# A transformer layer with dilated local attention: p\*v in 64x32 tiles with 32 queries by 48 keys, and a new order of all operations

## The chip, the cores and the metric

The kernel runs on one core of a Trainium2 chip. The core has five engines with a queue each: TensorE (PE, with its weight loads as PEld), VectorE (DVE), ScalarE (ACT), GpSimd (POOL) and SyncE (SP), which issues most DMAs. The metric is the device time of one execution in microseconds (us), where lower is better.

## What is computed

The input x has 2048 rows of 448 numbers in bf16. Attention has 16 heads of 28, and each query looks at 8 keys: its own position and the 7 that lie 2, 4, ... 14 positions back.

```python
def _A_ref(x, wqkv, wo):
    H = 16; Dh = D // H
    W, dil = 8, 2
    q, k, v = ...                                   # x @ wqkv, by heads
    idx = pos[:, None] - (jnp.arange(W) * dil)[None, :]
    mask = idx >= 0
    logits = jnp.einsum("bhsd,bhswd->bhsw", q, k[idx]) * Dh ** -0.5
    attn = softmax(where(mask, logits, -1e9))
    o = jnp.einsum("bhsw,bhswd->bhsd", attn, v[idx])
    return o.reshape(B, S, D) @ wo

def _B_ref(x, w1, w2, w3, w4):                      # F = 1792
    h = gelu(layernorm(x) @ w1)
    hs = concat(the four quarters of h's columns, shifted by +1, -1, +2, -2 rows) @ w2
    x1 = x + hs
    return x1 + gelu(layernorm(x1) @ w3) @ w4

h = x + _A_ref(layernorm(x), wqkv, wo)
return h + _B_ref(layernorm(h), w1, w2, w3, w4)
```

## The kernel before

The 2048 rows are worked on as four blocks of 512 rows (t = 0 to 3) of four tiles of 128 rows each. A block goes through these phases: **N1** (layernorm of x), **A1** (turning of the normalized rows, then q and k), **V** (v, and its copies to `vw`), **A2** (logits), **S** (softmax, and turning of p), **A3** (p\*v), **O** (times wo, plus x), **B1** (second layernorm) and **M** (times w1, gelu). Then five units of 2, 4, 4, 4 and 2 tiles go through **B2** (times w2 with shifted rows, layernorm as **T**), **W3** (times w3, gelu) and **B3** (times w4, output).

Each phase records its operations, and `arrange` then puts all 912 of them in the order of the list `ORDER`. Each engine executes its own operations strictly in that order, waiting on semaphores for the others. An operation that has an alternative runs on ACT, unless its number is in `OTHER`; then DVE runs it. Evictions from PSUM (`copy`) and normalizations by ACT have such alternatives. Buffers come from pools with fixed numbers: `NBD` for the spread p, `NLN` for normalized rows, `NACT` for turned rows, `NO` for output rows. `NORM`, `STATS` and `POWER` say for each block which engine ('a' ACT, 'v' DVE, 'p' POOL) does the normalizing, the statistics and the power -1/2 of a layernorm.

Most products have a contraction of 448 = 3 x 128 + 64, and are done as pairs of matmuls on the two halves of PE's rows (64x128 tiles). `duo` pairs two output banks: in the first half of the work (s = 0) the upper rows write bank A and the lower rows bank B, in the second half (s = 1) it is the other way round, since two row halves must not write one bank at the same time. That is why the second half waits for the first (`sdeps`). Turning in `transposed` and of p in `phase_A2` is split in two halves for the same reason.

p\*v: after the softmax, `pb` holds p with its 8 weights per query, spread so that turning it by PE gives `pt`, with keys on the partitions: 80 keys (16 before the tile's 64) by queries. For each of the four tiles of a block, DVE multiplies `pt`, broadcast, with a 0/1 mask (`bmask`), which gives `bd_r`: 80 keys by 64 queries for each of 32 (half tile, head) pairs. Then 32 matmuls with `vw` (80 keys by the 32 columns of one head) as weights and 64 columns of `bd_r` as moving operand write one bank, in four column tiles of 32. One eviction brings the bank, with reordered columns, into `actT`. `vw` is written by three or four DMAs per block from `vt`, issued on POOL's queue.

The loads of x, the attention's weights, w1 and w2 are issued by SP in the order in which they are recorded; those of w3 and w4 by POOL. All instructions show the line of the function that emits them (956), so they are told apart by the tiles that they write and read.

Of the kernel before, what the change touches and what calls it, by code (L numbers as in the profile page):

```python
# [6 lines left out]
ALU = mybir.AluOpType  # L7
# [6 lines left out]
NORM = {'N0': 'aava', 'N1': 'avvv', 'B1': 'avvv', 'B2': 'avvvv'}  # L14
STATS = {'N1': 'vvva', 'B1': 'vvav', 'B2': 'avvvv'}
NBD, NLN, NACT, NSM, NO = 3, 2, 4, 1, 3
# [34 lines left out]
"""  # L51
OTHER = """
96 110 502 548 595 596
"""

# [219 lines left out]
def bass_sequential_preLN__sliding_local_dilated__mixer_s_mlp__prompt_kernel(  # L275
# [11 lines left out]
    KW = 80  # L287
# [20 lines left out]
    with ExitStack() as es:  # L308
# [5 lines left out]
        bd_r = sb("bd_r", [KW, NBD, 2048], BF16)  # L314
        vt = sb("vt", [128, 2, 4, 512], BF16)
        vw = sb("vw", [KW, 2, 8, 512], BF16)
        bmask = sb("bmask", [KW, 64], BF16)
# [21 lines left out]
        pb = sb("pb", [128, NSM, NW * KW], BF16)  # L339
# [23 lines left out]
        pt = [arv(A_KV + t * KVB + 4 * KVW, KW, 1024) for t in range(NST)]  # L363
# [58 lines left out]
        def load_rows(chan, dst, src, lo, n, eng="sp", after=()):  # L422

            dma(chan, dst[:, 0:3, :], src[0:384, lo:lo + n].rearrange("(c k) n -> k c n", k=128), 384 * n * 2, eng=eng, after=after)
            return [dma("%sr%d" % (chan, h), dst[64 * h:64 * h + 64, 3, :], src[384:448, lo:lo + n], 64 * n * 2, eng=eng) for h in range(2)][-1]
# [4 lines left out]
        load_rows("wqk", wqkv_s[:, :, 0:2 * D], A_wqkv, 0, 2 * D)  # L430
        load_x(4, 2)
        load_x(6, 2)
        load_rows("wv", wqkv_s[:, :, 2 * D:3 * D], A_wqkv, 2 * D, D)
# [8 lines left out]
        for eng in ("sp", "pool"):  # L442
# [90 lines left out]
        def normalize(kind, i, out_ap, in_ap, summed=False, norm="v"):  # L533
# [6 lines left out]
            return dve("tensor_scalar", **by_dve)  # L540
# [14 lines left out]
        def doubled(ln, lo, n):  # L555
            dve("tensor_copy", out=ln(lambda v: v[:, lo:lo + n, D:512]), in_=ln(lambda v: v[:, lo:lo + n, 384:D]))

        def transposed(ln, how, n=4):
# [5 lines left out]
            w = n // 2  # L564
# [8 lines left out]
            first = []  # L573
            for s in range(2):
                for j in range(w):
                    op = steps([turn(h, j if h == s else w + j, c) for c in range(4) for h in range(2)], meth="transpose")
                    op.sdeps.update(first[-1:] * s)
                    first += [op] * (1 - s)
            for k, b in enumerate(banks):
                copy(a(lambda v, k=k: v[:, w * k:w * k + w, :, :]), b(lambda v: v.bitcast(BF16)[:, 0:512 * w].rearrange("p (i c n) -> p i c n", i=w, c=4)))  # L580
# [19 lines left out]
        def setup():  # L600
# [21 lines left out]
            for w in range(NW):  # L622
                bm = bmask[:].rearrange("p (m e r) -> p m e r", m=4, e=2)
                pool("affine_select", out=bm, in_=bm, pattern=[[16, 4], [1, 2], [DIL, NW]],
                     compare_op=ALU.not_equal, fill=1.0, base=PADK - DIL * w, channel_multiplier=-1)
# [11 lines left out]
        def phase_N1(t):  # L637
            ln = a1_ln[t] = _Tile(P_ln)
            step = 1 if t == 0 else 4
            summed = STATS["N1"][t] == "a"  # L640
            for lo in range(4 * t, 4 * t + 4, step):
# [7 lines left out]
                norms = norms_of("N1", t, 4) if t else NORM["N0"][lo]  # L649
# [5 lines left out]
        def phase_A1(t):  # L655
# [15 lines left out]
            names = ("q0", "q1", "q2", "k0", "k1", "k2")  # L671
# [21 lines left out]
        def phase_V(t):  # L693
# [16 lines left out]
            dma("vwa%d" % sl, vw[PADK:KW, sl, 0:8:2, :], vt[0:64, sl, :, :], 64 * 4096, "pool")  # L710
            dma("vwb%d" % sl, vw[0:KW, sl, 1:8:2, :], vt[48:128, sl, :, :], 80 * 4096, "pool")
            dma("vwc%d" % sl, vw[0:PADK, sl, 2:8:2, :], vt[112:128, sl, 0:3, :], 16 * 3072, "pool")

        def phase_A2(t):
# [31 lines left out]
            row = lambda v, off, step: bass.AP(v, off, [[v.shape[1] * v.shape[2], 128], [step, NW], [16, 4], [DIL, NW], [1, DIL]])  # L746
            dve("tensor_tensor", out=row(pb, sl * NW * KW + DIL, KW + DIL), in0=row(ls, sl * 512, 64),
# [10 lines left out]
            for g, b in enumerate(banks):  # L758
                copy(pt[t].rearrange("p (n r) -> p n r", r=NW)[:, :, 4 * g:4 * g + 4], b(lambda v: v[0:KW, :].rearrange("p (r n) -> p n r", r=4)))
# [238 lines left out]
```

## Time and profile before

| what | us |
|---|---|
| median of 3 runs (198.76 to 199.75) | 199.13 |
| the profiled execution, whole | 199.03 |
| its span, first to last instruction | 197.3 |
| PE busy | 186.4 (95% of the span) |
| DVE busy | 135.9 (69%) |
| ACT busy | 120.0 (61%) |
| POOL busy | 58.3 (30%) |

Busy times are unions of the instructions' durations. A matmul's duration runs from its start until its modelled end, which reaches into the matmuls behind it, so a busy PE isn't a PE at its peak. The clock granted to PE was 1.00 throughout.

### The profile page before, as it was taken

What the parts mean: (1) busy time and instruction counts of PE and PEld (TensorE: products, weight loads), DVE (VectorE), ACT (ScalarE), POOL (GpSimd) and SP (SyncE); (2) the same over time, 40 slices, a digit from 0 to 9 for tenths busy, and PEclk for the clock granted to TensorE, in tenths of its full rate; (3) what the DMA queues carried; (4) which work ended last, traced back from release to release, by engine and by line L of the source; (5) the groups of instructions that cost most, each with busy time, mean ns of one, the idle gap of its engine ahead of it and who ended that gap; (6) DMA issues with size and microseconds to landing.
All of it is one profiled execution on the core that took longest, in us unless ns stands there. A gap on an engine that the chain in (4) does not pass through costs nothing.

```text
span 197.3 us, 5852 instructions
## 1 busy us (share of the span) xinstructions
PE 186.4 (95%) x2532; PEld 97.6 (49%) x2532; DVE 135.9 (69%) x251; ACT 120.0 (61%) x271; POOL 58.3 (30%) x92
## 2 busy tenths in 40 slices
PE   6999998999999989999997999999996999999994
PEld 2474343544435455466553445555453454455672
DVE  4899999999999899999789836099571004302303
ACT  4869999999996989998270365720066023540350
POOL 4333430600002609726292460031076000610000
DMA  5979930370025360186508040004306100300211
GB/s 154 327 213 295 250 90 3 83 148 3 3 44 102 85 121 0 19 312 136 107 20 95 0 94 16 3 0 94 109 0 124 32 0 23 70 10 15 71 60 47
DMA packets 24513, 16.66 MB, mean 84 GB/s; under 512 B 16776, under 2 KB 23240, under 8 KB 24488
## 3 DMA queue, kind: packets, MB, share of 16 engines
q1 hardware_dynamic: 22872, 10.24, 22.5%
q0 software_dynamic: 1616, 6.05, 11.6%
q8 instruction: 20, 0.33, 0.7%
q14 instruction: 5, 0.04, 0.1%
HBM read 7.91 MB, written 1.84 MB: 49 GB/s over the span
## 4 chain that ended last, share of the span: by engine, by line
PE 48%; DVE 27%; ACT 10%; DMA 9%; issue 2%; POOL 1%; SPq 1%; DVEq 0%; POOLq 0%
PE ps L956 48%; DVE qk_r L956 8%; DVE lntm L956 6%; DMA actT<-lntm 5%; DVE bd_r L956 5%; ACT lntm L956 3%; DMA out_dram<-ost 3%; ACT actT L956 2%; ACT arena L956 2%; DVE st L956 2%; DVE arena L956 2%; DMA xin<-in_A_x_dram 1%; ACT vt L956 1%; POOL rs_y L956 1%; DVE ost L956 1%
## 5 line engine op out<-in xcount | busy, mean ns | idle before, releaser
L956 PE MATMUL ps<-actT,arena 64*128 64x512 bf16 (+1 forms) x742 | 70.4, 332 | 4.2 <-DMA actT<-lntm 3.8
L956 ACT ACTIVATE h3T<-ps 128x512 bf16<-128x512 f32 (+1 forms) x70 | 30.7, 521 | 52.6 <-PE ps L956 52.4
L956 PEld LDWEIGHTS ps<-actT,arena 64*128 64x128 bf16 x742 | 34.6, 94 | 34.5 <-DMA actT<-lntm 4.4
L956 PE MATMUL ps<-arena,h3T 64*128 64x448 bf16 (+2 forms) x434 | 45.4, 343 | 0.0
L956 DVE SCALAR_TENSOR_TENSOR ost<-ps,mrs,arena 128x448 bf16<-128x448 f32 (+1 forms) x17 | 10.9, 651 | 38.7 <-PE ps L956 33.7
L956 ACT ACTIVATE arena<-ps 128x512 bf16<-128x512 f32 (+4 forms) x70 | 33.1, 510 | 6.5 <-PE ps L956 5.7
L956 PEld LDWEIGHTS ps<-arena,h3T 64*128 64x128 bf16 (+1 forms) x434 | 23.6, 94 | 18.3 <-ACT h3T L956 0.2
L956 DVE TENSOR_TENSOR qk_r<-arena 128x4096 bf16<-128x4096 bf16 (+1 forms) x16 | 31.7, 2013 | 0.4 <-ACT arena L956 0.3
L956 POOL TENSOR_TENSOR arena<-arena,xin 128x448 f32<-128x448 f32 x16 | 20.0, 1272 | 18.3 <-DVE lntm L956 18.3
L956 POOL TENSOR_TENSOR rs_y<-rs_x,mhalf 128x4 f32<-128x4 f32 (+1 forms) x9 | 9.3, 1035 | 44.9 <-DVE rs_x L956 44.8
L956 ACT ACTIVATE actT<-ps 128x512 bf16<-128x512 f32 (+2 forms) x27 | 17.6, 691 | 3.9 <-PE ps L956 3.6
L956 DVE TENSOR_TENSOR bd_r<-arena,bmask 80x2048 bf16<-80x2048 bf16 x16 | 18.9, 1214 | 0.0
L956 DVE SCALAR_TENSOR_TENSOR arena<-xin,rs_y,ps 128x448 f32<-128x448 bf16 x16 | 10.4, 669 | 10.3 <-PE ps L956 10.3
L956 POOL TENSOR_TENSOR mrs<-nm,rs_y 128x4 f32<-128x4 f32 x4 | 8.4, 2102 | 27.1 <-ACT rs_y L956 21.9
L956 DVE BATCH_NORM_STATS2 st<-xin 128x6 f32<-128x448 bf16 x24 | 13.9, 612 | 2.0 <-DMA xin<-in_A_x_dram 1.8
L956 PE MATMUL ps<-wo_s,actT 64*128 64x448 bf16 x128 | 14.7, 350 | 0.2 <-ACT xin L956 0.2
L956 PE MATMUL ps<-w_s,arena 64*128 64x448 bf16 (+1 forms) x128 | 14.3, 349 | 0.0
L956 PE MATMUL ps<-actT,w_s 64*112 64x512 bf16 x112 | 13.5, 377 | 0.3 <-DMA actT<-lntm 0.3
L956 POOL DMA_DIRECT2D vw<-vt x15 | 9.1, 606 | 14.5 <-PE ps L956 9.4
L956 PE MATMUL ps<-arena,actT 64*128 64x448 bf16 x112 | 13.1, 350 | 0.1
L956 DVE TENSOR_SCALAR lntm<-arena,mv,rs_y 128x448 bf16<-128x448 f32 x14 | 9.2, 699 | 3.1 <-POOL rs_y L956 3.1
L956 PEld LDWEIGHTS ps<-actT,w_s 64*112 64x112 bf16 x112 | 7.4, 127 | 4.3 <-ACT actT L956 0.4
(74 smaller groups left out, 178.3 us busy)
## 6 DMA issues: line engine op xcount, KB each, us to landing
out_dram<-ost SPq DMA_DIRECT2D x15, 112.0 KB, 1.8
arena<-in_B_w_dram POOLq DMA_DIRECT2D x1, 1568.0 KB, 8.1
arena<-in_B_w_dram POOLq DMA_DIRECT2D x1, 1344.0 KB, 7.3
vw<-vt POOLq DMA_DIRECT2D x4, 320.0 KB, 3.9
vw<-vt POOLq DMA_DIRECT2D x4, 256.0 KB, 4.0
xin<-in_A_x_dram SPq DMA_DIRECT2D x2, 448.0 KB, 5.8
xin<-in_A_x_dram SPq DMA_DIRECT2D x3, 224.0 KB, 4.7
arena<-in_A_wqkv_dram SPq DMA_DIRECT2D x1, 672.0 KB, 5.3
```

Of the source, the lines that this page charges most:

```text
L956: inst = getattr(eng, meth)(**kw)
```

## The change

p\*v is cut differently. A block of 64 queries by 80 keys becomes two blocks of 32 queries by 48 keys (16 before, 32 own), one on the partitions 0 to 47, the other on 64 to 111. PE works on them as 64x32 tiles, eight side by side: two row halves, each into its own bank, by four column tiles. `bd_r` now has 128 partitions and holds two tiles of 128 rows per buffer, so a block has two spreading operations instead of four, and two groups of 128 matmuls with 32 columns instead of four groups of 32 matmuls with 64. The matmuls' moving operand is read in the order in which the eviction wants it, and the evictions copy runs of 32 columns, one per row half. p is turned with 128 columns of weights. `vw` is written by five or six DMAs per block.

The turns (of layernorm output and of p) write one bank per row half, and no longer wait between halves. v's weights are loaded first. The pairs of q and k are formed anew. The number of `bd_r` buffers goes from 3 to 2 and of output buffers from 3 to 5. All normalizations have ACT as their first choice, and the statistics of B1 of the first block are done by ACT (sums of squares). The first four tiles are normalized in two pairs instead of one by one. `ORDER` is new, and 41 operations run on DVE by `OTHER` instead of 6.

```diff
-NORM = {'N0': 'aava', 'N1': 'avvv', 'B1': 'avvv', 'B2': 'avvvv'}
-STATS = {'N1': 'vvva', 'B1': 'vvav', 'B2': 'avvvv'}
-NBD, NLN, NACT, NSM, NO = 3, 2, 4, 1, 3
+NORM = {'N0': 'aaaa', 'N1': 'aaaa', 'B1': 'aaaa', 'B2': 'aaaaa'}
+STATS = {'N1': 'vvva', 'B1': 'avav', 'B2': 'avvvv'}
+NBD, NLN, NACT, NSM, NO = 2, 2, 4, 1, 5
...
 OTHER = """
-96 110 502 548 595 596
+99 110 115 125 209 210 211 235 236 237 238 266 301 304 329 331 332 356 357 358 380 421 445 474 493 531 563 564 565 566
+587 588 595 652 654 655 729 801 803 866 867
 """
+FIRST = ((0, 2), (2, 2))
+RQ = 'sp'
+RV = 'act'
...
-    KW = 80
+    QB = 32
+    KB = PADK + QB
...
-        load_rows("wqk", wqkv_s[:, :, 0:2 * D], A_wqkv, 0, 2 * D)
+        load_rows("wv", wqkv_s[:, :, 2 * D:3 * D], A_wqkv, 2 * D, D, last=RV)
+        load_rows("wqk", wqkv_s[:, :, 0:2 * D], A_wqkv, 0, 2 * D, last=RQ)
         load_x(4, 2)
         load_x(6, 2)
-        load_rows("wv", wqkv_s[:, :, 2 * D:3 * D], A_wqkv, 2 * D, D)
...
             def turn(h, il, c):
-                b = banks[il // w]
                 part = (TOP, BOT)[h]
-                return (h, dict(out=b(lambda v, lo=il % w * 512 + c * 128 + 64 * h: v.bitcast(BF16)[:, lo:lo + 64]),
+                return (h, dict(out=banks[h](lambda v, lo=(4 * il + c) * 64: v.bitcast(BF16)[:, lo:lo + 64]),
                                 in_=ln(lambda v, il=il, c=c: v[part, il, 128 * c:128 * c + 128]), identity=ident[part, part]), 64)
...
-                op.sdeps.update(first[-1:] * s)
...
-            names = ("q0", "q1", "q2", "k0", "k1", "k2")
+            names = ("q0", "k0", "q1", "k1", "q2", "k2")
...
-            dma("vwa%d" % sl, vw[PADK:KW, sl, 0:8:2, :], vt[0:64, sl, :, :], 64 * 4096, "pool")
-            dma("vwb%d" % sl, vw[0:KW, sl, 1:8:2, :], vt[48:128, sl, :, :], 80 * 4096, "pool")
-            dma("vwc%d" % sl, vw[0:PADK, sl, 2:8:2, :], vt[112:128, sl, 0:3, :], 16 * 3072, "pool")
+            for name, to, even, lo, hi in (("a", PADK, 0, 0, QB), ("b", 64, 0, PADK, 64), ("c", 0, 1, 64 - PADK, 64 + QB), ("d", 64, 1, 64 + PADK, 128)):
+                dma("vw%s%d" % (name, sl), vw[to:to + hi - lo, sl, even:8:2, :], vt[lo:hi, sl, :, :], (hi - lo) * 4096, "pool")
+            dma("vwe%d" % sl, vw[0:PADK, sl, 2:8:2, :], vt[112:128, sl, 0:3, :], 16 * 3072, "pool")
...
-            first = steps([turn(h, h, r) for r in range(4) for h in range(2)])
-            steps([turn(h, 1 - h, r) for r in range(4) for h in range(2)]).sdeps.add(first)
+            steps([turn(h, r) for r in range(NW) for h in range(2)])
...
-            for il in range(4):
+            for pair in range(2):
                 bd = _Tile(P_bd)
-                b = _Tile(P_bank)
-                dve("tensor_tensor", block=True, out=bd(lambda v: v.rearrange("p (n g r) -> p n g r", g=8, r=NW)),
+                banks = [_Tile(P_bank), _Tile(P_bank)]
+                dve("tensor_tensor", block=True, out=bd(lambda v: v.rearrange("p (n g r) -> p n g r", g=4, r=NW)),
...
+                at = (i8 // 2 * 8 + 2 * c + i8 % 2) * QB
+                specs.append((("matmul", dict(out=banks[half](lambda v, j=j, at=at: v[32 * j:32 * j + 32, at:at + QB].rearrange("p (m r e) -> p m r e", m=2, e=DIL)),
+                                              lhsT=vw[part, sl, 4 * pair + i8, (4 * c + j) * 32:(4 * c + j) * 32 + 32],
+                                              rhs=bd(lambda v, part=part, lo=(16 * i8 + 4 * c + j) * QB: v[part, lo:lo + QB].rearrange("p (m e r) -> p m r e", m=2, e=DIL)), start=True, stop=True)),
+                              (QB, "q", 4 * half + j)))
...
-                copy(a(lambda v, il=il: v[:, il, :, :].rearrange("p c n -> p (c n)").rearrange("p (m r e) -> p m r e", r=NW, e=2)),
-                     b(lambda v: v.rearrange("p (m e r) -> p m r e", r=NW, e=2)))
+                for half, b in enumerate(banks):
+                    copy(a(lambda v, lo=2 * pair, half=half: v[:, lo:lo + 2, :, :].rearrange("p i c (u h q) -> p (i c u) h q", u=2, h=2)[:, :, half, :]),
+                         b(lambda v: v.rearrange("p (u q) -> p u q", q=QB)))
```

More of the change, by code (lines that the diff above doesn't have):

```diff
@@ L313, in bass_sequential_preLN__sliding_local_dilated__mixer_s_mlp__prompt_kernel @@
         qk_r = sb("qk_r", [128, 2, 4096], BF16)
-        bd_r = sb("bd_r", [KW, NBD, 2048], BF16)
+        bd_r = sb("bd_r", [128, NBD, 2048], BF16)
         vt = sb("vt", [128, 2, 4, 512], BF16)
-        vw = sb("vw", [KW, 2, 8, 512], BF16)
-        bmask = sb("bmask", [KW, 64], BF16)
+        vw = sb("vw", [128, 2, 8, 512], BF16)
+        bmask = sb("bmask", [128, QB], BF16)
         lntm = sb("lntm", [128, NLN, 4, 512], BF16)
@@ L338, in bass_sequential_preLN__sliding_local_dilated__mixer_s_mlp__prompt_kernel @@
         indj = ls[:, NSM - 1, 0:40].bitcast(BF16).rearrange("p (c h) -> p c h", c=5)
-        pb = sb("pb", [128, NSM, NW * KW], BF16)
+        pb = sb("pb", [128, NSM, NW * 128], BF16)
         ost = sb("ost", [128, NO, D], BF16)
@@ L362, in bass_sequential_preLN__sliding_local_dilated__mixer_s_mlp__prompt_kernel @@
         kr = [arv(A_KV + t * KVB + 3 * KVW, 128, PADK + 256) for t in range(NST)]
-        pt = [arv(A_KV + t * KVB + 4 * KVW, KW, 1024) for t in range(NST)]
+        pt = [arv(A_KV + t * KVB + 4 * KVW, 128, 1024) for t in range(NST)]
         maskrow = arv(A_KV + (NST - 1) * KVB, 1, 512)
@@ L420, in load_x, with load_rows @@
             return dma("x%d" % i, xin[:, i:i + n, :], xv[:, i:i + n, :], 128 * n * D * 2)
-        def load_rows(chan, dst, src, lo, n, eng="sp", after=()):
+        def load_rows(chan, dst, src, lo, n, eng="sp", after=(), last=None):
             dma(chan, dst[:, 0:3, :], src[0:384, lo:lo + n].rearrange("(c k) n -> k c n", k=128), 384 * n * 2, eng=eng, after=after)
-            return [dma("%sr%d" % (chan, h), dst[64 * h:64 * h + 64, 3, :], src[384:448, lo:lo + n], 64 * n * 2, eng=eng) for h in range(2)][-1]
+            return [dma("%sr%d" % (chan, h), dst[64 * h:64 * h + 64, 3, :], src[384:448, lo:lo + n], 64 * n * 2, eng=last or eng) for h in range(2)][-1]
         S.tag = "load"
@@ L441, in bass_sequential_preLN__sliding_local_dilated__mixer_s_mlp__prompt_kernel @@
         dma("w4", w4_s, B_w4.rearrange("(f k) n -> k f n", k=128), D * F * 2, eng="pool", after=[late])
-        for eng in ("sp", "pool"):
+        for eng in ("sp", "pool", "act"):
             loads = [op for op in S.ops if op.tag == "load" and op.eng == eng]
@@ L539, in normalize @@
                              alts=[("dve", [("tensor_scalar", by_dve)])])
-            return dve("tensor_scalar", **by_dve)
+            return dve("tensor_scalar", True, **by_dve)
         def norms_of(kind, t, n):
@@ L555, in doubled @@
         def doubled(ln, lo, n):
-            dve("tensor_copy", out=ln(lambda v: v[:, lo:lo + n, D:512]), in_=ln(lambda v: v[:, lo:lo + n, 384:D]))
+            dve("tensor_copy", True, out=ln(lambda v: v[:, lo:lo + n, D:512]), in_=ln(lambda v: v[:, lo:lo + n, 384:D]))
         def transposed(ln, how, n=4):
@@ L563, in transposed @@
                 return a
-            w = n // 2
             banks = [_Tile(P_bank), _Tile(P_bank)]
             def turn(h, il, c):
-                b = banks[il // w]
                 part = (TOP, BOT)[h]
-                return (h, dict(out=b(lambda v, lo=il % w * 512 + c * 128 + 64 * h: v.bitcast(BF16)[:, lo:lo + 64]),
+                return (h, dict(out=banks[h](lambda v, lo=(4 * il + c) * 64: v.bitcast(BF16)[:, lo:lo + 64]),
                                 in_=ln(lambda v, il=il, c=c: v[part, il, 128 * c:128 * c + 128]), identity=ident[part, part]), 64)
[L573 to L576, printed above, removed]
-                    op.sdeps.update(first[-1:] * s)
-                    first += [op] * (1 - s)
-            for k, b in enumerate(banks):
-                copy(a(lambda v, k=k: v[:, w * k:w * k + w, :, :]), b(lambda v: v.bitcast(BF16)[:, 0:512 * w].rearrange("p (i c n) -> p i c n", i=w, c=4)))
+            for il in range(n):
+                steps([turn(h, il, c) for c in range(4) for h in range(2)], meth="transpose")
+            for h, b in enumerate(banks):
+                copy(a(lambda v, lo=64 * h: v[:, 0:n, :, lo:lo + 64]), b(lambda v: v.bitcast(BF16)[:, 0:256 * n].rearrange("p (i c n) -> p i c n", i=n, c=4)))
             return a
@@ L621, in setup @@
             pool("memset", ap=bmask[:], constant=0.0)
[L622 to L625, printed above, removed]
+            bm = bmask[:].rearrange("p (m e r) -> p m e r", m=2, e=2)
+            for base in [64 * half + PADK - DIL * w for half in range(2) for w in range(NW)]:
+                pool("affine_select", out=bm, in_=bm, pattern=[[16, 2], [1, 2], [DIL, NW]],
+                     compare_op=ALU.not_equal, fill=1.0, base=base, channel_multiplier=-1)
             pool("memset", ap=gT[:, :, 0:2], constant=0.0)
@@ L638, in phase_N1 @@
             ln = a1_ln[t] = _Tile(P_ln)
-            step = 1 if t == 0 else 4
             summed = STATS["N1"][t] == "a"
-            for lo in range(4 * t, 4 * t + 4, step):
+            for lo, step in FIRST if t == 0 else ((4 * t, 4),):
                 for i in range(lo, lo + step):
@@ L648, in phase_N1 @@
                     sums_stats(0, range(lo, lo + step), lambda i: xin[:, i, :], ln, lo % 4)
-                norms = norms_of("N1", t, 4) if t else NORM["N0"][lo]
+                norms = norms_of("N1", t, 4) if t else NORM["N0"][lo:lo + step]
                 rstd(0, lo, step, summed, norms, POWER["N1"][t])
@@ L745, in phase_A2, with turn @@
             dve("reciprocal", out=zs[:, sl, :], in_=zs[:, sl, :])
-            row = lambda v, off, step: bass.AP(v, off, [[v.shape[1] * v.shape[2], 128], [step, NW], [16, 4], [DIL, NW], [1, DIL]])
-            dve("tensor_tensor", out=row(pb, sl * NW * KW + DIL, KW + DIL), in0=row(ls, sl * 512, 64),
-                in1=bass.AP(zs, sl * 64, [[64 * NSM, 128], [8, NW], [2, 4], [0, NW], [1, DIL]]), op=ALU.mult)
+            row = lambda v, off, step, half: bass.AP(v, off, [[v.shape[1] * v.shape[2], 128], [step, NW], [half, 2], [16, 2], [DIL, NW], [1, DIL]])
+            dve("tensor_tensor", out=row(pb, sl * NW * 128 + DIL, 128 + DIL, 64), in0=row(ls, sl * 512, 64, QB),
+                in1=bass.AP(zs, sl * 64, [[64 * NSM, 128], [8, NW], [4, 2], [2, 2], [0, NW], [1, DIL]]), op=ALU.mult)
             banks = [_Tile(P_bank), _Tile(P_bank)]
-            def turn(h, g, r):
+            def turn(h, r):
                 part = (TOP, BOT)[h]
-                return (h, dict(out=banks[g](lambda v: v[0:KW, 128 * r + 64 * h:128 * r + 64 * h + 64]),
-                                lhsT=pb[part, sl, (4 * g + r) * KW:(4 * g + r + 1) * KW], rhs=ident[part, part], start=True, stop=True), 64)
-            first = steps([turn(h, h, r) for r in range(4) for h in range(2)])
-            steps([turn(h, 1 - h, r) for r in range(4) for h in range(2)]).sdeps.add(first)
-            for g, b in enumerate(banks):
-                copy(pt[t].rearrange("p (n r) -> p n r", r=NW)[:, :, 4 * g:4 * g + 4], b(lambda v: v[0:KW, :].rearrange("p (r n) -> p n r", r=4)))
+                return (h, dict(out=banks[h](lambda v: v[:, 64 * r:64 * r + 64]), lhsT=pb[part, sl, r * 128:(r + 1) * 128], rhs=ident[part, part],
+                                start=True, stop=True), 64)
+            steps([turn(h, r) for r in range(NW) for h in range(2)])
+            for h, b in enumerate(banks):
+                copy(pt[t].rearrange("p (n r) -> p n r", r=NW)[:, 64 * h:64 * h + 64, :], b(lambda v: v.rearrange("p (r n) -> p n r", r=NW)))
         def phase_A3(t):
@@ L763, in phase_A3 @@
             sl = t % 2
-            for il in range(4):
+            for pair in range(2):
                 bd = _Tile(P_bd)
-                b = _Tile(P_bank)
-                dve("tensor_tensor", block=True, out=bd(lambda v: v.rearrange("p (n g r) -> p n g r", g=8, r=NW)),
-                    in0=pt[t][:, il * 256:il * 256 + 256].rearrange("p (n r) -> p n r", r=NW).unsqueeze(2).broadcast_to([KW, 32, 8, NW]),
-                    in1=bmask[:].rearrange("p (g r) -> p g r", r=NW).unsqueeze(1).broadcast_to([KW, 32, 8, NW]), op=ALU.mult)
-                mms([(b(lambda v, j=j, lo=128 * c + 64 * a2: v[32 * j:32 * j + 32, lo:lo + 64]),
-                      vw[:, sl, 2 * il + a2, (4 * c + j) * 32:(4 * c + j) * 32 + 32],
-                      bd(lambda v, lo=(16 * a2 + 4 * c + j) * 64: v[:, lo:lo + 64]), True, True, 64, j)
-                     for c in range(4) for a2 in range(2) for j in range(4)])
-                copy(a(lambda v, il=il: v[:, il, :, :].rearrange("p c n -> p (c n)").rearrange("p (m r e) -> p m r e", r=NW, e=2)),
-                     b(lambda v: v.rearrange("p (m e r) -> p m r e", r=NW, e=2)))
+                banks = [_Tile(P_bank), _Tile(P_bank)]
+                dve("tensor_tensor", block=True, out=bd(lambda v: v.rearrange("p (n g r) -> p n g r", g=4, r=NW)),
+                    in0=pt[t][:, pair * 512:pair * 512 + 512].rearrange("p (n r) -> p n r", r=NW).unsqueeze(2).broadcast_to([128, 64, 4, NW]),
+                    in1=bmask[:].rearrange("p (g r) -> p g r", r=NW).unsqueeze(1).broadcast_to([128, 64, 4, NW]), op=ALU.mult)
+                specs = []
+                for i8 in range(4):
+                    for c in range(4):
+                        for half in range(2):
+                            for j in range(4):
+                                part = slice(64 * half, 64 * half + KB)
+                                at = (i8 // 2 * 8 + 2 * c + i8 % 2) * QB
[3 more added lines that the diff above has]
+                                              (QB, "q", 4 * half + j)))
+                S.group("pe", [x for x, _ in specs], pe=[y for _, y in specs])
+                for half, b in enumerate(banks):
+                    copy(a(lambda v, lo=2 * pair, half=half: v[:, lo:lo + 2, :, :].rearrange("p i c (u h q) -> p (i c u) h q", u=2, h=2)[:, :, half, :]),
+                         b(lambda v: v.rearrange("p (u q) -> p u q", q=QB)))
```

62 rows, old and new, of the table ORDER are left out of this document.

## The prediction

> **What bounds the kernel now.** I read the page's busy shares, then busy time by stage, then the chain that ended last, then groups, waits and the timeline at the steps that change. First the page: share of the span and count per engine, and the span in 40 slices of 4.93 us.
>
> ```profile
> span 197.3 us, 5852 instructions
> ...
> PE 186.4 (95%) x2532; PEld 97.6 (49%) x2532; DVE 135.9 (69%) x251; ACT 120.0 (61%) x271; POOL 58.3 (30%) x92
> ...
> PE   6999998999999989999997999999996999999994
> ...
> DVE  4899999999999899999789836099571004302303
> ACT  4869999999996989998270365720066023540350
> ```
>
> PE's 95% overstates: the streaming time of its matmuls (2.38 columns a ns, as 512-column matmuls on one tile follow each other every 215 ns, divided by the tiles that run side by side) sums to 172 us. Until slice 18 (about 90 us) DVE and ACT are as full as PE. By stage (PE, PEld, DVE, ACT, POOL busy, each with its count):
>
> ```profile
> 8.75:35.42 26.67, 25.82 (x359) 12.46 (x361) 26.09 (x42) 23.85 (x58) 8.89 (x29) 1.00 0.61 172
> 35.42:65.99 30.57, 29.66 (x574) 14.19 (x571) 30.28 (x48) 28.33 (x63) 5.52 (x11) 1.00 0.33 66
> 65.99:91.56 25.57, 24.70 (x428) 14.24 (x430) 24.56 (x39) 23.62 (x59) 15.40 (x11) 1.00 0.42 110
> ...
> 108.42:149.70 41.28, 41.01 (x401) 21.32 (x403) 26.15 (x57) 17.72 (x32) 12.73 (x13) 1.00 0.17 38
> ```
>
> In the three attention stages (to 91.56 us, where the last block's p is turned) DVE is busy 81 of 83 us and ends most waits. After 108 us PE alone is full. The chain (start, us, what) says the same and shows the two places where late PE waits:
>
> ```profile
> 33.00 3.40 DVE bd_r L956 x3
> ...
> 101.98 6.39 DMA actT<-lntm
> ...
> 136.61 2.66 DMA out_dram<-ost
> ...
> 140.00 2.46 DMA out_dram<-ost
> ...
> 148.96 4.29 DMA actT<-lntm
> ...
> 153.29 40.75 PE ps L956 x441
> ```
>
> At 106.1 and 149.7 us PE runs out of matmuls for 1.6 and 2.3 us until a transposing DMA lands. The second is late because DVE stood waiting for output buffers before its layernorm.
>
> **The change, part by part.** Groups and timeline give the prices:
>
> ```profile
> L956 DVE TENSOR_TENSOR bd_r<-arena,bmask 80x2048 bf16<-80x2048 bf16 x16 | 18.9, 1214 | 0.0
> L956 PE MATMUL ps<-bd_r,vw 80*32 80x64 bf16 x512 | 6.2, 195 | 0.5 <-DVE bd_r L956 0.5
> ```
> ```profile
> 30.79 0.74 PE L956 MATMUL ps<-ident,pb 64*80 64x64 bf16 x16 [0.33 <-DVE pb L956]
> 41.02 0.42 PE L956 MATMUL ps<-bd_r,vw 80*32 80x64 bf16 x32 [0.24 <-DVE bd_r L956]
> 41.37 0.74 PE L956 MATMUL ps<-arena,actT 64*128 64x448 bf16 x6
> ```
> ```profile
> DVE ost L956 <- DMA out_dram<-ost: 5.1, 4, 1.8
> ```
>
> *Spreading p (bd).* 16 DVE instructions become 8 of the same 2048 elements per partition. Queued one behind another they cost 3.40/3 = 1.135 us each: -9.1 us of DVE, 6 of the 8 before the last p.
>
> *p\*v on PE.* 512 matmuls of 64 columns become 1024 of 32. Now four tiles start every 28.3 ns (32 matmuls in 0.23 us, then 0.12 us until other tiles start at 41.37): 7.1 ns each, 3.6 us in all. After, eight tiles could by columns alone start every 14 ns (1.8 us in all). But the records in a group lie 1.6 to 1.7 ns apart, a weight load and a matmul 3.3 to 3.5: 16 instructions need 27 to 28 ns. I take 3.5 ns each, 3.6 us: no change. Bounds: 1.8 us, and 14.7 us if each took the 14.4 ns of the 64-wide transposes; 7.1 ns, as now, makes 7.3. "TensorEngine Tiling (Array Packing)", Performance Considerations, Instruction Overhead, in the Trainium skill, speaks against the split: under some 60 columns a matmul gets no shorter. By it 128 groups of eight take 3.6 us and not 1.8.
>
> *Fewer drains.* A change between tile shapes costs about 0.115 us (the 0.12 above; the same at 35.4 and 37.2). Along PE's order I count 47 changes before, 37 after: -1.1 us. Turning p writes both row halves into one bank, so its second half waits: 16 matmuls span 0.54 us between first and last start where 14 steps of 20 ns make 0.28. A bank per row half takes away five such waits of 0.24 us (p and layernorm turns), and the order leaves 4 instead of 8 pairs of one matmul group's halves adjacent: about -2 us. 128 weight columns instead of 80 in p's turns lower 20 ns to the 14.4 of the other turns: -0.4 us. Most of this lies before the last p, where DVE binds; I credit only what lies behind it, -0.35 us.
>
> *Moves between DVE and ACT.* Before the last p is written, DVE loses 6 bd (-6.8 us), 4 bn_stats and bn_aggr (-2.5, B1 of t = 0 by ACT's sums), 4 normalizes (-1.2), 4 xb that the order puts later (-2.4) and small ones (-0.3), and gains 8 evictions (+4.5) and 6 nmr (+0.4): 82.8 to 74.6 us, -8.2. ACT loses 8 evictions (-4.0), 4 gelus that move behind (-1.9), and small ones, and gains 3 normalizes (+2.0) and the sums (+0.8): 78.9 to 74.3 us with its table loads. A normalize is 0.65 us there against 0.31 on DVE. The evictions of turned tiles, of p and of p\*v keep their sizes and number and only step differently: no change.
>
> *Order.* PE has 76.0 us of matmuls before its last p turn, after the change 69.8: 6.1 us of w2 and w3 go behind it. Behind it PE has 104.1 us instead of 98.2.
>
> *Loads.* v's 336 KB now stand before q/k's on SP's queue, though PE still takes q/k first. x and q/k landed by 8.1 us with DMA at some 330 GB/s, so +1.0 us at the start. The two v remainders go out on ACT behind two normalizes: nobody waits, v is wanted after 15 us. The first four tiles are normalized in pairs: two Ln and Exp pairs fewer on ACT, about as long as the wait for the second tile that they add; I cost it at nothing, since q/k weights land later than either.
>
> *POOL.* 23 vw issues instead of 15 at 0.61 us, +4.9 us, and 8 more bmask selects of at most 0.42 us. POOL is idle enough (30%). But its 1344 KB w3 load, issued at 13.9 us before, now stands behind three vw issues that wait for the v evictions (about 25 us), and the last vw of t = 0 behind it. With 7.3 us to land, vw is there at 33 to 35 us; its bd is due at 37. Hidden, by 2 us; if that cover is gone the loss is up to 3 us.
>
> *Five output buffers* instead of three remove DVE's 5.1 us of waits, so the last 4-tile layernorm is ready before PE: -2.3 us. The wait at 106.1 us stays: the chain after the last p (2 bd, 4 xb, stats, power 1.0, norms, DMA 4.3 to 6.4) is 12 to 14 us against 12 us of matmuls.
>
> *The sum.* The last p is written at 90.4 us; -8.2 (DVE) +1.0 (loads) = 83.2. ACT is then busy 74.3 of 82 us (91%, before 78.9 of 87), and PE has room. The turn starts 1.1 us later as now: 84.3. From there PE took 105.7 us for 98.2 of matmuls; 7.5 over, less 2.3 and 0.35, on 104.1 makes 109.0. Span 193.3; with the 1.7 around it (199.03 - 197.3) 195.0 us against the profiled 199.03, which is 0.1 under the median of 199.13.
>
> **The rivals.**
>
> *p\*v too slow: slower.* p's rows are now read as moving operand with neighbours 8 elements (16 bytes) apart; every matmul in this trace reads runs. If a column costs k times its 0.44 ns (28.3/64), p\*v takes 1.8k us: k = 2 is hidden under the 3.6 us taken, k = 8 makes 14.5 us, +10.9 and 206 us. It turns to slower (over 200.1) from k = 5, 8.7 ns a matmul. For it: no row shows such a read. Against: the q\*k sums scatter into PSUM at 54 ns per matmul, the full rate. Chance 0.20. "SBUF — State Buffer" (section "Door 1: The DMA port swizzle", the note on cachelines) in the Trainium skill says that each access to a new 16-byte line pays a penalty, without a figure; no run here shows it yet.
>
> *ACT takes DVE's place: about no change.* Both stand at 91%, and each waits for the other at every softmax. If half of the 8.2 us is lost so: 195.0 + 4.1 = 199.1 us. For it: ACT's 28.3 of 30.6 us in the middle stage. Against: before, DVE at 98% cost ACT little. Chance 0.13.
>
> *All drains count and PE's groups of eight run by columns: faster still.* -1.8 (p\*v), -1.6 (the wait at 106 us gone), -1.0 (drains): 190.6 us. The page's instruction rule is against its first term. Chance 0.12.
>
> **How the numbers follow.** The forecast, 195.0 with 192 to 197.5 of its own, has 0.55. A measurement of this kernel tells about 0.5%, 1 us. Faster (under 198.1): 0.55 + 0.12 + 0.03 of the second rival = 0.70; within: 0.09; slower: the first rival with its tail of lost cover, 0.21. The range leaves out 0.07 below and 0.13 above: 190.5 to 202.5.
>
> **What would show it.** Right: bd x8 near 1.2 us; 128 p\*v matmuls in 0.45 us; the last pb ending at 82 to 85 us; no wait on out_dram before the last layernorms; no gap of 2 us near 145 to 150 us. Wrong: p\*v spaced over 8 ns, pb ending after 88 us, or first q/k matmuls after 11 us.

## The result and the profile after

The changed kernel is slower: 218.39 us median of 4 runs (216.06 to 224.81) against 199.16 us for the kernel before beside it, a ratio of 1.092 [1.083, 1.102]. The forecast was 195.0. The profiled execution took 224.81 us, the longest of the four; the other three have spans of 214 to 217 us and granted clocks of 0.945 to 0.96 against its 223.0 and 0.923, so the losses below are somewhat larger than the median's.

The page after, the same rows as before, and two that before had nothing to tell (the granted clock, and the queue that fetches instructions):

```profile
span 223.0 us, 6917 instructions
...
PE 199.6 (90%) x3044; PEld 111.0 (50%) x3044; DVE 126.8 (57%) x246; ACT 125.0 (56%) x280; POOL 54.5 (24%) x108
...
PE   7597999469996997799947999999999999999995
...
DVE  5677999487395599197772187127788204300402
ACT  3549999626895297488924434747605640270160
...
PEclk9999999755997699589995899999999999999999
...
q8 instruction: 24, 0.39, 0.8%
```

DVE is 9.1 us less busy. But every engine now has holes until slice 21 (about 119 us), PE too, and the clock falls in the same stretch: from 42.2 to 55.7, 69.5 to 76.2, 90.0 to 96.7 and 117.3 to 124.0 us it was granted at 0.50. From 119 us on PE is full, as before. The queue q8 brought 24 pages of 16 KB in place of 20: 1024 more PE instructions are four pages of 256.

Stages of 10 us, from the part in which PE had been 97% full and just behind it (PE, PEld, DVE, ACT, POOL busy, then clock):

```profile
40.00:50.00 10.00, 5.08 (x248) 2.58 (x245) 6.65 (x9) 4.01 (x8) 5.39 (x14) 0.61 0.57 119
50.00:60.00 10.00, 10.00 (x158) 5.62 (x158) 5.78 (x6) 7.01 (x15) 1.13 (x1) 0.71 0.50 169
...
70.00:80.00 10.00, 9.85 (x74) 3.67 (x74) 5.62 (x17) 5.11 (x12) 2.29 (x4) 0.69 0.39 80
...
90.00:100.00 10.00, 9.40 (x93) 4.17 (x95) 5.22 (x10) 6.89 (x17) 0.00 (x0) 0.66 0.43 54
...
110.00:120.00 10.00, 5.53 (x291) 4.10 (x288) 7.30 (x19) 3.65 (x9) 1.34 (x3) 0.86 0.01 3
```

A row such as 50:60 reads as PE busy for all of 10 us, at 0.71 of its clock: full, and not at its peak. The chain that ended last names the new thing, a wait called "issue", in which an engine waits for nothing that the profile shows:

```profile
42.42 1.24 DVE bd_r L962
...
47.73 1.95 issue
...
68.43 1.72 issue
...
87.83 2.77 issue
...
112.87 2.17 issue
116.28 2.31 issue
118.58 101.16 PE ps L962 x1043
```

Five such waits, 10.9 us in the chain. The timeline of PE (start, us, what, idle before) shows that one of them cuts a group of p\*v matmuls in two, with no releaser in sight:

```profile
43.74 1.22 PE L962 MATMUL ps<-bd_r,vw 48*32 48x32 bf16 x128 [2.97 <-DVE bd_r L962]
...
47.10 0.62 PE L962 MATMUL ps<-bd_r,vw 48*32 48x32 bf16 x55
49.68 0.78 PE L962 MATMUL ps<-bd_r,vw 48*32 48x32 bf16 x73 [1.95 <-issue]
```

I numbered PE's instructions in the trace, weight loads, matmuls and semaphore instructions together. The five waits stand before instructions 1217, 2241, 3009, 3777 and 4033: they are 1024, 768, 768 and 256 apart, all multiples of 256, which is one fetched page. From entering a page until the first instruction of the next could run, these five took 3.6 to 5.4 us. In the kernel before no page passed in under 3.15 us, and no wait over 0.25 us stood at a page's end. A group of 128 p\*v matmuls is a whole page, and PE uses it up in about a microsecond. The packets of q8 in the trace fit: before each of the five waits a fetch began 1.1 to 2.6 us after PE had entered the page before, landed at 48.14, 68.76, 89.10, 113.78 and 117.21 us, and PE went on 1.2 to 1.5 us behind the landing. A short page alone makes no wait: the one from instruction 2497 on was used up in 2.52 us, and PE went straight on, for the next page's fetch had begun at 83.06 us, ahead of this page's own start at 84.01. "Runtime: NRT & Kernel Launch", Instruction fetch mechanics, in the Trainium skill states blocks of 16 KiB with 256 instructions for such a fetch, which agrees with these distances; it also calls the cost of crossing a boundary "mostly hidden", and here it was 1.7 to 2.8 us, five times.

### The profile page after: what moved, and what is told of

The parts are those of the page before. It is cut to its first block, busy times and chain, and to the rows that moved or that the text cites. A ratio compares the mean times of both kernels' runs of the same rounds, so it can differ in the third digit from the quotient of the medians.

```text
span 223.0 us, 6917 instructions
## 1 busy us (share of the span) xinstructions
PE 199.6 (90%) x3044; PEld 111.0 (50%) x3044; DVE 126.8 (57%) x246; ACT 125.0 (56%) x280; POOL 54.5 (24%) x108
## 4 chain that ended last, share of the span: by engine, by line
PE 72%; ACT 7%; issue 6%; POOL 5%; DMA 5%; SPq 2%; DVE 1%; POOLq 0%; DVEq 0%
PE ps L962 72%; DMA xin<-in_A_x_dram 5%; POOL bmask L962 3%; ACT arena L962 3%; SPq L962 2%; ACT lntm L962 2%; POOL vw L962 2%; ACT vt L962 1%; ACT actT L962 1%; ACT L962 1%; DVE bd_r L962 1%; DVE ost L962 1%; POOLq L962 0%; ACT rs_y L962 0%; ACT rs_x L962 0%
## 5 line engine op out<-in xcount | busy, mean ns | idle before, releaser
L962 PE MATMUL ps<-actT,arena 64*128 64x512 bf16 (+1 forms) x742 | 73.7, 343 | 1.6 <-DMA arena<-in_A_wqkv_dram 1.3
L962 PEld LDWEIGHTS ps<-actT,arena 64*128 64x128 bf16 x742 | 38.1, 98 | 32.6 <-issue 4.1
L962 ACT ACTIVATE arena<-ps 128x512 bf16<-128x512 f32 (+3 forms) x68 | 31.6, 516 | 8.6 <-PE ps L962 8.2
L962 POOL TENSOR_TENSOR arena<-arena,xin 128x448 f32<-128x448 f32 x16 | 16.7, 1057 | 44.0 <-DVE lntm L962 31.6
L962 POOL DMA_DIRECT2D vw<-vt x23 | 13.2, 579 | 40.4 <-ACT vt L962 25.0
L962 PE MATMUL ps<-bd_r,vw 48*32 48x32 bf16 x1024 | 10.3, 198 | 12.5 <-issue 9.5
L962 PE MATMUL ps<-wo_s,actT 64*128 64x448 bf16 x128 | 18.5, 419 | 0.0
L962 PEld LDWEIGHTS ps<-bd_r,vw 48*32 48x32 bf16 x1024 | 9.0, 91 | 16.0 <-issue 13.4
L962 DVE TENSOR_TENSOR bd_r<-arena,bmask 128x2048 bf16<-128x2048 bf16 x8 | 9.7, 1222 | 6.0 <-POOL bmask L962 3.2
L962 PE MATMUL ps<-qk_r,zc 128*32 128x512 bf16 x128 | 11.0, 452 | 0.6 <-DVE qk_r L962 0.6
```

Source lines behind the costliest of these rows:

```text
L962: inst = getattr(eng, meth)(**kw)
```

## The experiments

**1. Only more instructions, in the kernel before.**

```diff
-      mms([(b(lambda v, j=j, lo=128 * c + 64 * a2: v[32 * j:32 * j + 32, lo:lo + 64]),
+      mms([(b(lambda v, j=j, lo=128 * c + 64 * a2 + 32 * x: v[32 * j:32 * j + 32, lo:lo + 32]),
...
-            for c in range(4) for a2 in range(2) for j in range(4)])
+            for c in range(4) for a2 in range(2) for x in range(2) for j in range(4)])
```

> The kernel before, with each 64-column matmul of p*v written as two of 32 columns: 1024 matmuls and 1024 weight loads instead of 512 and 512, same columns, same reads, same order. Instruction supply (TensorE's instructions come in pages of 256 and a page that is used up in less than some 3 us leaves the engine empty): gaps of 1 to 3 us with nothing to wait for, at distances that are multiples of 256 instructions, where two p*v groups stand side by side; 204 to 211 us. Rival, p's strided read: nothing is strided here, so only the pace of 8 ns per matmul counts, at most 512 x 8 = 4 us and no gaps: 199 to 203 us. Rival, the order of bmask and loads: it is as before, 199 us.

Measured: 210.77 us, 1.056 [1.048, 1.064]. Nothing of the change is in it but the count of p\*v matmuls: same columns, same runs read, same order, same DVE work. PE's waits show it:

```profile
PEld ps L956 <- issue: 17.1, 44, 2.7
```

Before, these were 5.7 us with 0.7 as the longest. Waits of 1.38, 1.36 and 2.76 us (here and below from one start on PE to the next) stand at instructions 1217, 1985 and 4289, with a shorter one of 0.55 us at 4033, again multiples of 256 apart, and p\*v is spaced 8.1 to 8.7 ns though its moving operand is read in runs. So 512 more instruction pairs cost 11.6 us by themselves, within what was expected of instruction supply.

**2. The changed kernel with half the count.** Each matmul takes 64 columns of the spread p, so 512 in place of 1024.

```diff
-                for i8 in range(4):
+                for i8 in (0, 2):
```

> The kernel after, with 512 p*v matmuls of 64 columns in place of 1024 of 32: the same columns through the same eight tiles with the same stride. It leaves out the right weights and mask block for every second pair of a half tile (the first one's are used for both). Instruction supply: 1024 fewer instructions, the gaps without a releaser go, and the clock drops behind them; 201 to 207 us. Rival, the strided read: the same columns are read in the same way, 216 to 218 us, and p*v still takes 1 us per group. Rival, the order of bmask and loads: unchanged, 214 to 218 us.

Measured: 199.25 us, 1.000 [0.996, 1.004]. Of the five page waits two are left (2.15 and 2.11 us). The spacing stays at 8.1 to 8.5 ns with twice the columns: in a long group the pace goes by instructions, not by columns. With the start as it is, 19 us hang on the count, more than the 11 to 17 us expected.

**3. and 4. The order of the start.** In the first the last twelve mask selects on POOL go ahead of the first `vw` copies, in the second q/k's weights are loaded ahead of v's; both move numbers in `ORDER`, and the second swaps the two `load_rows` lines.

> The kernel after, with the last 12 mask selects on POOL placed ahead of the first vw issues; nothing else. Order as the cause: the 3.2 us in which the first spreading waits for the mask go, with the low clock behind them, 4 to 8 us less: 210 to 214 us. Instruction supply as the cause: 1 to 3 us less, 215 to 217 us, since the gaps of the p*v groups stay.

> The kernel after, with the weights of q and k loaded ahead of those of v, as before the change; nothing else. Order as the cause: the first q/k matmuls start 1 to 1.5 us earlier than 10.9 us and the second x tiles too, 2 to 4 us less: 214 to 216 us. Instruction supply as the cause: at most 1 us less, 217 to 218 us.

Measured: 217.39 us (1.081 [1.070, 1.093]) and 215.51 us (1.070 [1.061, 1.080]). The first shows one wait hidden behind another. Its chain has no mask in it, but:

```profile
31.93 10.48 DMA vw<-vt
```

The last `vw` copies share POOL's queue with the 1344 KB of w3 issued between them, and land 8 to 11 us after their issue. The page waits stay in both. The second time lies in the range expected if the order were the cause, the first just above the one for instruction supply: these two runs alone don't tell the two causes apart.

**5. The start mended in all three places.** q/k's weights first, masks first, and w3 behind the five `vw` copies of the first block (`ORDER` again).

> The changed kernel with the order of its start mended and nothing else: q/k weights loaded ahead of v's, the twelve late mask selects ahead of the first vw copies on POOL, and the 1344 KB of w3 behind the five vw copies of the first tile. Instruction supply (main theory): the gaps of 2 to 3 us at multiples of 256 instructions stay, so only the start is won back: the 3 us of q/k first, the 1 us of the masks, and some 2 us because vw no longer lands 8 to 11 us after its issue: 211 to 214 us. If the order of loads were the main loss: below 203 us.

Measured: 211.83 us, 1.051 [1.041, 1.061]. The first p\*v group starts at 38.51 in place of 43.74 us. The start was worth 6.6 us; the waits at page ends remain (1.11, 2.38, 2.07, 2.44 and 2.18 us and one of 0.62, all multiples of 256 apart). One page that was used up in 2.08 us ran through here; the wait of 2.18 us stands at the end of the page behind it.

**6. and 7. The groups spread out.** All 1024 matmuls stay, each group of 128 becomes four of 32, with at least 1.2 us of other PE work between two; first on the changed kernel, then with the start mended.

```diff
-                specs = []
                 for i8 in range(4):
+                    specs = []
                     for c in range(4):
...
-                S.group("pe", [x for x, _ in specs], pe=[y for _, y in specs])
+                    S.group("pe", [x for x, _ in specs], pe=[y for _, y in specs])
```

> The changed kernel, all 1024 p*v matmuls kept, but each group of 128 written as four groups of 32 (by i8), and at least 1.2 us of other TensorE work put between two of them; the work that depends on p*v moves behind its last piece. Every page of 256 instructions then lasts 3.3 us or more by the columns of its matmuls, most over 4 us. Instruction supply: the gaps of 2 to 3 us shrink to a few tenths, the clock stays up, the time falls by 12 us of gaps and some 5 us of clock to 199 to 204 us, although the p*v matmuls are as many and as slow (8 ns). A cost in the p*v matmuls themselves (their strided read, their weights, a change of shape between groups): 32 groups in place of 8 make it no faster, 216 us or more.

> Both edits together: the p*v groups in four pieces with other work between, and the order of the start mended. If instruction supply and the start are the two losses and they add: 194 to 199 us, as fast as the kernel before or a little faster. If one hides the other: 199 to 204 us, as with the pieces alone.

Measured: 254.82 and 251.44 us, 1.275 [1.267, 1.282] and 1.259 [1.250, 1.268]. The time was missed by 50 us and more, yet the mechanism did what was expected: in the first the longest wait at a page's end was 0.24 us, and a matmul took 4.1 to 4.5 ns. The clock, expected to stay up, did not: it was granted at 0.926 and 0.919 on average in the two profiled executions. The timeline of PE shows what took the place of the page waits:

```profile
61.54 0.32 PE L963 MATMUL ps<-bd_r,vw 48*32 48x32 bf16 x32
61.79 1.93 PE L963 MATMUL ps<-actT,arena 64*128 64x512 bf16 x14
63.64 0.32 PE L963 MATMUL ps<-bd_r,vw 48*32 48x32 bf16 x32
63.89 1.05 PE L963 MATMUL ps<-qk_r,zc 128*32 128x512 bf16 x16
66.91 0.61 PE L963 MATMUL ps<-qk_r,zc 128*32 128x512 bf16 x8 [1.97 <-DVE qk_r L963]
```

The pieces run through; but the work put between them comes earlier than its operands, and what needs p\*v comes some 10 us later, block after block. In the stretch from 75 to 116 us, starts on PE lie up to 3.16, 4.63 and 2.39 us apart before such work, and once 2.43 us where the trace names no releaser (not at a page's end).

**8. Half the count and the start mended.**

> The kernel with 512 p*v matmuls of 64 columns (it leaves out the second pair's own weights and mask) with the order of the start mended as well. It shows what the halved DVE work is worth where the instruction count is that of before. Main theory: 199.3 less 4 to 6 us of the start: 193 to 196 us, the forecast's own sum. If the DVE work was not what bound the first half: 198 to 200 us.

Measured: 197.30 us, 0.982 [0.973, 0.991]. That is neither the 193 to 196 us of the main theory nor the 198 to 200 of its rival, and the interval, some 195 to 199 us beside a kernel before of 200.65, reaches into both. Between 5 and 8 lies only the count: 14.5 us. Page waits of 0.89, 1.74 and 1.74 us are left in 8. The last `pb` ends at 84.73 us, where the forecast had 83.2.

**9. Five output buffers alone, in the kernel before.**

```diff
-        P_o = _Pool("o", lambda k: ost[:, k, :], NO)
+        P_o = _Pool("o", lambda k: ost[:, k, :] if k < NO else vt[:, 0, k - NO, 0:D], NO + 2)
```

> The kernel before with five output buffers in place of three (the two more lie in the part of vt that no tile reads any longer) and nothing else changed: one part of the change alone. The term of the prediction for it was 2.3 us: the waits of the vector engine for a free output buffer go, and with them TensorE's gap in the last third: 196 to 198 us. If TensorE was waiting there for something else: 199 us, no change.

Measured: 196.75 us in 6 runs, 0.982 [0.977, 0.987], as expected: 1.8% less than the kernel before. No wait on `out_dram` is left, and the chain's end shows the late gap gone:

```profile
135.21 4.26 DMA actT<-lntm
139.61 52.67 PE ps L956 x553
```

Before, the transfer started at 148.96 and PE ran without a break only from 153.29.

**10. A narrower spread.** As 7, with one step of PE work (0.3 us) between the pieces.

> The changed kernel with the order of the start mended and the p*v groups in four pieces as before, but with only one step of other TensorE work (some 0.3 us) between two pieces, so that little is moved. By the columns, seven of the eight pages that hold p*v last 1.5 to 3.1 us, so instruction supply leaves part of the gaps: 4 to 6 us of them in place of 10, and the work behind p*v is moved by 1 to 3 us in place of some 10: 203 to 208 us, faster than the order alone (211.8) and far faster than the wide spread (251.4). If the wide spread was slow because of the pieces themselves (32 groups, each a change of shape for TensorE) and not because of what was moved behind them: 230 us or more, with TensorE's own groups longer.

Measured: 221.55 us, 1.105 [1.097, 1.112]. Again a miss, and again the page waits nearly vanish: no more than 0.83 us at one boundary, some 2 us in all, against 10.8 in 5. The pieces themselves can't be the whole cost, since 32 groups stand in 7 as well and the two differ by 30 us. They are not free either: the trace has 32 stretches of p\*v where 5 has 6, and at the prediction's 0.115 us for a change of tile shape 26 more make some 6 us (an estimate). Output projections, put right behind the last piece, now wait for that piece's eviction, six times for 1.2 to 2.5 us from one start on PE to the next, 9.8 us in all:

```profile
42.47 0.93 PE L963 MATMUL ps<-wo_s,actT 64*128 64x448 bf16 x8 [1.46 <-ACT actT L963]
...
50.56 0.56 PE L963 MATMUL ps<-wo_s,actT 64*128 64x448 bf16 x2 [1.30 <-ACT actT L963]
```

What else the order of these three kernels costs was not taken apart further.

**11. and 12. The DVE saving by itself, and with the split.** Both are number 9 with half of the spreading operations on DVE; the second has the edit of number 1 as well.

```diff
-                bd = _Tile(P_bd)
+                if il % 2 == 0:
+                    bd = _Tile(P_bd)
...
-                dve("tensor_tensor", block=True, out=bd(...
+                if il % 2:
+                    dve("memset", ap=scr[:, 4 * t + il:4 * t + il + 1], constant=0.0)
+                else:
+                    dve("tensor_tensor", block=True, out=bd(...
```

> The kernel before with five output buffers, and with eight of its sixteen spreading operations on DVE replaced by a memset of one element (left out: every second tile of 128 rows uses the spread p of its neighbour). TensorE's instructions and the order are unchanged. It prices the DVE step of the prediction by itself: eight times 1.135 us less on DVE, six of them before the last p. If DVE sets the pace of the attention stages: 196.75 less 5 to 7 us, 190 to 192 us. If ACT or the order takes its place at once: 194.5 to 197 us.

> The kernel just named, with each p*v matmul of 64 columns written as two of 32 as well: the DVE saving of the change and its 1024 matmuls, in the order of the kernel before. If the instruction cost of the split is about what it was in the kernel before (11.6 us) and adds: 11 to 12 us over the run with 512 matmuls, 201 to 204 us. If the DVE saving makes p*v groups come closer together, pages run out faster: 14 us or more over it.

Measured: 196.05 us, 0.981 [0.972, 0.989], and 205.54 us, 1.024 [1.014, 1.035]. Beside number 9's 0.982 the DVE saving is worth nothing that these runs can tell; the time lies in the range for "ACT or the order takes its place". The stages of number 11 (35 to 66 and 66 to 91 us):

```profile
35.00:66.00 31.00, 30.11 (x582) 14.47 (x575) 26.46 (x48) 28.74 (x64) 5.51 (x11) 1.00 0.32 65
66.00:91.00 25.00, 24.04 (x420) 13.69 (x422) 21.77 (x38) 23.34 (x58) 9.20 (x11) 1.00 0.40 109
```

Number 9 has 30.21 and 24.01 on PE there, and 30.77 and 23.92 on DVE. DVE lost 6.5 us, PE nothing, and the last `pb` moved from 90.86 to 90.38. DVE's waits between 30 and 91 us grew from 1.1 to 7.5 us, 3.4 of them for PE and 3.2 for ACT. The chain of number 11 shows two places where PE holds it:

```profile
57.63 3.83 PE ps L961 x44
61.49 0.69 DVE mx L961
...
72.99 12.30 PE ps L961 x172
85.31 0.70 DVE mx L961
```

The softmax begins when PE has worked through its queue. Between 49.99 and 57.59 us the same chain runs on ACT. Number 12 adds 9.5 us for the split, less than the 11 to 12 expected, with waits of 0.74, 1.34, 0.68 and 2.36 us at instructions 1217, 1985, 4033 and 4289, the places of number 1.

## Why the prediction was wrong

From 218.39 back to the forecast's 195.0 there are 23.4 us. The runs divide them: the start 6.6 (the changed kernel against 5), the count of p\*v instructions 14.5 (5 against 8), and 2.3 left. By the ratios to the kernel before that ran beside each, they are 8.3, 13.8 and 0.5; each is sure to some 2 or 3 us, so what is left can't be told from nothing.

- **"I take 3.5 ns each, 3.6 us: no change" failed, and cost most.** The price came from groups of 32 matmuls. In groups of 128 the first 32 start some 4.1 ns apart and all later ones 8.3 (below), 8.0 over the group: 1024 by 4.5 ns is 4.6 us more. That lies within the bounds given. What the sum had no term for is the supply of instructions: five page waits, 10.9 us in the chain. It had none for the clock either, which stood at 0.50 for 33.6 us in four stretches, each beginning while PE waited, where it had been 1.00. "TensorE: Matmul & The Clock Gate", Part 1, in the Trainium skill ties this clock to how busy PE has been of late; the rows agree in place, but not after every wait (in number 5 two waits of over 2 us left the next stretch at 1.00), and no edit here moves the clock alone.
- **What the clock is worth can be estimated from the record.** The granted clock of each execution is known, and span times clock hardly differs between the executions of a kernel: 205.1 to 206.1 us for the four executions of the changed kernel, whose spans run from 214.3 to 223.0, and 196.8 to 198.1 us for the kernel before, with spans from 196.9 to 199.9. So lost clock costs about its whole share of the span. By this estimate the changed kernel would be 8.3 us slower than the kernel before at an equal clock, and some 11 of its 19 us go with the clock. Of the 14.5 us between 5 and 8 (203.3 and 194.1 us, on average), about 9 are not the clock's and about 5 are. The 9 fit the two profiles, in which page waits differ by 6.4 us (10.8 and 4.4) and the pace of 512 matmuls by 4.1. The split alone costs, at an equal clock, 8.6 us in number 1 and 8.3 in number 12. That the waits bring the low clock about is not shown.
- **The rival that forecast slower named the wrong mechanism.** A strided moving operand doesn't set the pace: number 1 reads runs and has 8.1 to 8.7 ns in its long groups, and number 6 reads with strides at 4.1 to 4.5. A price of the stride that stays under this pace can't be seen here. The price from which it was to decide, 8.7 ns a matmul, was not even reached.
- **The instruction rule of "TensorEngine Tiling (Array Packing)"** in the Trainium skill was drawn on only for the length of a matmul, 128 groups of eight in 3.6 us. At 8.0 ns a matmul they took 8.2 us: in long groups eight pairs of weight load and matmul need 66 ns, more than twice the 28 ns taken. So the first term of the third rival, groups of eight that run by columns, is out as well.
- **"Hidden, by 2 us; if that cover is gone the loss is up to 3 us."** The cover was gone. POOL's chain of `vw` issues and selects ran from 29.4 to 42.4 us, where the last select released the first `bd`; DVE had sat idle before it for 3.2 us. The price was about right, but not the place: the prediction had looked for the loss in the landing of `vw`. That lay hidden behind the selects, and number 3 won only 1.0 us.
- **Loads, +1.0 us.** The first q/k matmuls began at 10.89 us against 8.75, so +2.1; q/k first gave back 2.9.
- **"-8.2 (DVE)": the size was about right, its worth is not shown.** `bd` took 1.22 us, eight times, and in number 8 the last `pb` ended at 84.73. But the new order gets there by moving PE work behind it, and number 8's tail is 111.6 us (196.3 - 84.73), where the forecast had 109.0. Number 8 is as fast as five output buffers alone (0.982 each), yet it holds 4.4 us of page waits and number 9 none, so what the rest of the change would be worth without them stays open. In the order of the kernel before, number 11 gives the answer: time taken off DVE turned into waits of DVE. That DVE "ends most waits" was read as a bound; it was one of three engines almost equally full (from 35 to 66 us in number 9: DVE 30.77, PE 30.21, ACT 28.76 of 31 us). The rival "ACT takes DVE's place" was nearer to this than the forecast: there the whole saving was lost, to PE as much as to ACT.
- **Right:** the five output buffers (-2.3 forecast; alone -3.0 between the medians, -2.5 by span times clock), no wait on `out_dram` before the last layernorms, no gap before the last unit, and a full PE, though only from 119 us on: two page waits, 2.17 and 2.31 us, still stand behind the last p.
- **A reading.** 106.1 and 149.7 us, where the prediction has PE run out, are the starts of the last group before each wait. PE stood idle until 108.42 and 153.29, for 1.40 and 2.10 us.

Of the signs named, two were at their edges (spacing 8.0 ns, first q/k 10.89 us) and the third far over: the last `pb` ended at 106.36 us.

## What to carry to other kernels

Count the instructions that an engine uses up per microsecond, not their durations alone: a change that halves the size of many small operations doubles the rate at which instructions must arrive, and where pages are used up faster than the next ones come, a wait for "issue" shows at multiples of that page. It need not stand behind the shortest page: one that was fetched early runs through. Compare executions at the same granted clock before dividing up a loss. Where several engines are over 90% busy, price a saving on one by taking it out alone: here 6.5 us of DVE work gave nothing. And in an order written for given lengths a long operation can't be cut up freely: spreading it removed the page waits, and the time still rose by 10 to 40 us.

## What the runs showed of the hardware

- Within a group of 128 pairs of weight load and matmul, eight matmuls start in 32 to 33 ns up to the 32nd (the first eight in 30 to 49), and in 66 to 67 ns from about the 40th on: 64 instructions at 2 ns each, then 4.2 ns each. A granted clock of 0.50 left this unchanged (the group at 43.74 us in the changed kernel). Groups of 32 (number 6) stay at 31 to 49 ns throughout. With 64 columns in place of 32 the later pace is the same (66 to 68 ns for eight).
- Pages of 256 PE instructions are fetched one by one, each 16 KB in 0.9 to 1.5 us in the changed kernel, and where PE ran dry 3.6 to 5.4 us had passed since it entered the page before. Pages used up in 2.52 us (the changed kernel) and 2.08 us (number 5) ran through.
- The granted clock falls to 0.50 in stretches of 3.4 us or a multiple (6.8 and 13.7 us in the changed kernel), and over the executions of one kernel span times granted clock stayed within 1 to 1.3 us for the changed kernel and the kernel before (205.1 to 206.1 and 196.8 to 198.1 us).
- Small copies on POOL's queue behind the 1344 KB load took 8 to 11 us to land (number 3); the medians of the `vw` copies by size are 3.7 to 5.1 us in the changed kernel.
